# All eight PSUM banks in one ring, tiled products merged into seven runs a batch, evictions spread over slots

## The chip, the cores and the metric

The kernel runs on one core of one Trainium2 chip. The metric is device time in microseconds (us) of a whole execution. Medians are of several executions. TensorE is PE in the profile, VectorE DVE, ScalarE ACT, GpSimd POOL; PEld is the weight load.

## The reference

Eight batches, eight heads, 576 positions. `phi` gives, through a softmax over the positions, 32 memory slots a head; attention runs from `q` to those slots; its output goes through a bilinear feed-forward layer.

```python
a = softmax(phi, axis=seq)                       # 8 x 8 x 576 x 32
k_m, v_m = einsum('bhsm,bhsd->bhmd', a, k), einsum('bhsm,bhsd->bhmd', a, v)
x = softmax(scale * q @ k_m.T) @ v_m             # to 4608 x 512
out = ((x @ w_a) * (x @ w_b)) @ w_out            # d_ff 1536, out 4608 x 512 float32
```

## The kernel before

TensorE writes its products to PSUM, which this kernel uses as eight banks. An eviction is the copy of a bank to SBUF by ACT or DVE; after it the bank can be used again. A ring hands its banks out in turn.

For each batch the kernel multiplies `v_m` into `w_a` and `w_b` first (the "folds", which write `vab`), so the up products work on the 32-slot weights of each head. A batch is prepared by small products on parts of the TensorE array: sums over positions (`pkv`), transposes (`pT`), scores, denominators (`pD`), folds (`pva`). They are slipped between the full-array products of the batch before: `up` (pa, pb) and `down` (po). I call the up loops of batches 0 to 7 the first to eighth loop, and the piece between the second and the third loop, where batch 2 is finished with down products alone as filler, the stretch.

```python
ps_up = ctx.enter_context(tc.tile_pool(name="ps_up", bufs=2, space=bass.MemoryType.PSUM))   # pa, pb: 2 banks each
ps_any = ctx.enter_context(tc.tile_pool(name="ps_any", bufs=1, space=bass.MemoryType.PSUM)) # 4 banks in a ring
# ...
def fold(lo, hi, z, on_act=(True, False)):
    pvas = [banks.tile([P, 512], F32, name="pva") for _ in range(2)]
    for j in range(4):
        for g in range(2):
            nc.tensor.matmul(pvas[g][32 * j:32 * j + 32, 0:hi - lo], ..., tile_position=(64 * r, 32 * j))
    for g in range(2):      # evicted at once, one on ACT, one on DVE
        ...
# ...
for x in "qt2 sc0 qt3 sc1 va0a va0b dn va1a va1b nr0 va2a nr1 va2b nr2 - nr3 -".split():   # the stretch
    run(2, x)
    work.advance(2)         # two down products after each
every = "qt0 exp0 qt1 exp1 qt2 kv0 kv1 - kvt sc0 qt3 sc1 - va0a dn va0b nr0 va1a nr1 va1b nr2 va2a nr3 va2b"
for b in range(2, B):
    ups(steps(b, 0, NFF), named(b + 1, every) if b + 1 < B else (), (work.ready - work.done) / (2 * NFF))
```

The softmax here doesn't subtract the row's maximum and nothing guards it: scores larger than these inputs give would overflow.

## Time and profile before

| what | value |
|---|---|
| device time, median | 270.53 us (270.46 to 270.94, 3 runs) |
| span of the profile | 268.7 us |
| PE busy | 258.4 us, 96% |
| DVE, ACT busy | 62%, 50% |
| first product of the second, third loop | 55.26, 85.48 us |
| last product ends (its start plus 0.216 us), span ends | 263.3, 268.65 us |

The PE share counts products that overlap (a down product lasts 0.38 us on average, and the next can start 0.216 us after it). So it says that PE seldom stands without work, but not what PE spends. That is read from starts: the difference between two starts in the timeline is what a product or a run of products costs.

### The profile page before, as it was taken

What the parts mean: (1) busy time and instruction counts of PE and PEld (TensorE: products, weight loads), DVE (VectorE), ACT (ScalarE), POOL (GpSimd) and SP (SyncE); (2) the same over time, 40 slices, a digit from 0 to 9 for tenths busy, and PEclk for the clock granted to TensorE, in tenths of its full rate; (3) what the DMA queues carried; (4) which work ended last, traced back from release to release, by engine and by line L of the source; (5) the groups of instructions that cost most, each with busy time, mean ns of one, the idle gap of its engine ahead of it and who ended that gap; (6) DMA issues with size and microseconds to landing.
All of it is one profiled execution on the core that took longest, in us unless ns stands there. A gap on an engine that the chain in (4) does not pass through costs nothing.

```text
span 268.7 us, 7200 instructions
## 1 busy us (share of the span) xinstructions
PE 258.4 (96%) x2912; PEld 138.9 (52%) x2912; DVE 166.4 (62%) x366; ACT 135.4 (50%) x331; POOL 36.5 (14%) x59
## 2 busy tenths in 40 slices
PE   8979989999999999999999999999999999999992
PEld 3435553446534655655555545555565555666540
DVE  7544864479857679855885477846884577444100
ACT  3126752278454565726663645646573564544220
POOL 8943332100210310121003100000000000000000
PEclk9998999999999999999999999999999999999999
DMA  7999999999993595169515971111111111112243
GB/s 159 195 198 207 253 207 224 236 295 232 217 204 90 130 189 117 41 139 208 117 25 154 187 159 41 39 41 41 39 41 40 43 41 39 40 41 67 62 109 78
DMA packets 25858, 33.50 MB, mean 125 GB/s; under 512 B 1888, under 2 KB 20320, under 8 KB 25824
## 3 DMA queue, kind: packets, MB, share of 16 engines
q0 software_dynamic: 19536, 23.01, 47.6%
q1 hardware_dynamic: 6288, 10.03, 14.7%
q8 instruction: 23, 0.38, 0.5%
q14 instruction: 11, 0.09, 0.1%
HBM read 42.47 MB, written 9.44 MB: 193 GB/s over the span
## 4 chain that ended last, share of the span: by engine, by line
PE 84%; DMA 10%; DVE 2%; issue 1%; POOL 1%; ACT 1%; ACTq 0%; DVEq 0%; POOLq 0%
PE po L385 34%; PE pa L455 19%; PE pb L464 17%; DMA wb_sb<-in_moe_w_b_dram 6%; PE pva L341 6%; DMA kv_sb<-in_v_dram 4%; PE pkv L216 2%; PE pscore L296 2%; PE pR L327 1%; PE pT L245 1%; PE pD L315 1%; PE pT L251 1%; POOL q_sb L90 1%; DVE qT L203 1%; DVE ht L467 0%
## 5 line engine op out<-in xcount | busy, mean ns | idle before, releaser
L385 PE MATMUL po<-wo_sb,ht 128*128 128x512 f16 x432 | 120.4, 379 | 0.0
L467 DVE TENSOR_TENSOR ht<-a_sb,pb 128x288 f16<-128x288 f16 x192 | 77.9, 446 | 35.1 <-PE pb L464 31.2
L458 ACT CAST a_sb<-pa 128x288 f16<-128x288 f32 x192 | 67.7, 407 | 35.7 <-PE pa L455 35.2
L455 PE MATMUL pa<-A,vab 128*128 128x288 f16 x384 | 64.1, 289 | 0.5 <-ACT a_sb L458 0.5
L464 PE MATMUL pb<-A,vab 128*128 128x288 f16 x384 | 63.8, 288 | 0.3
L385 PEld LDWEIGHTS <-ht 128*128 128x128 f16 x432 | 40.8, 98 | 24.2 <-issue 2.5
L351 ACT CAST vab<-pva 128x512 f16<-128x512 f32 (+1 forms) x54 | 29.5, 555 | 43.0 <-PE pva L341 42.7
L455 PEld LDWEIGHTS <-vab 128*128 128x128 f16 x384 | 33.0, 98 | 25.2 <-issue 11.8
L464 PEld LDWEIGHTS <-vab 128*128 128x128 f16 x384 | 35.2, 98 | 18.2 <-ACT vab L351 1.2
L353 DVE CAST vab<-pva 128x512 f16<-128x512 f32 x46 | 31.6, 688 | 8.4 <-PE pva L341 7.9
L394 ACT ACTIVATE o_sb<-po 128x512 f32<-128x512 f32 (+1 forms) x36 | 21.8, 605 | 21.0 <-PE po L385 21.0
L305 ACT ACTIVATE E<-pscore,rphi 128x288 f16<-128x288 f32 x32 | 14.3, 497 | 25.3 <-PE pscore L296 25.3
L203 DVE STREAM_TRANSPOSE qT<-q_sb 128x576 f16<-128x576 f16 x32 | 24.0, 763 | 0.0
L330 DVE SCALAR_TENSOR_TENSOR A<-E,rphi,pR 128x288 f16<-128x288 f16 x32 | 16.0, 512 | 8.2 <-PE pR L327 7.5
L341 PEld LDWEIGHTS <-kvT 64*32 64x32 f16 x400 | 6.0, 89 | 19.3 <-issue 18.1
L119 PE MATMUL pw<-warm 128*128 128x512 f16 (+1 forms) x48 | 13.4, 415 | 1.3 <-DVE warm L113 1.3
L78 POOL DMA_DIRECT2D phi_sb<-in_phi_dram x7 | 5.3, 755 | 67.4 <-ACT exp_sb L194 35.5
L319 DVE RECIPROCAL rD<-pD 128x144 f16<-128x144 f32 x8 | 8.4, 1056 | 6.9 <-PE pD L315 6.8
L231 DVE CAST kvm<-pkv 128x128 f16<-128x128 f32 (+1 forms) x16 | 4.0, 265 | 13.3 <-PE pkv L216 13.3
L194 ACT ACTIVATE exp_sb<-phi_sb 128x576 f16<-128x576 f32 x16 | 10.9, 696 | 2.6 <-DMA phi_sb<-in_phi_dram 2.6
L341 PE MATMUL pva<-wa_sb,kvT 64*32 64x512 f16 (+1 forms) x200 | 10.5, 378 | 0.3 <-DVE rD L319 0.3
L341 PE MATMUL pva<-wb_sb,kvT 64*32 64x512 f16 (+1 forms) x200 | 10.6, 382 | 0.1
(44 smaller groups left out, 108.0 us busy)
## 6 DMA issues: line engine op xcount, KB each, us to landing
out_dram<-o_sb SPq DMA_DIRECT2D x72, 128.0 KB, 2.4
kv_sb<-in_v_dram POOLq DMA_DIRECT2D x8, 576.0 KB, 10.3
phi_sb<-in_phi_dram POOLq DMA_DIRECT2D x7, 576.0 KB, 5.7
kv_sb<-in_k_dram POOLq DMA_DIRECT2D x7, 576.0 KB, 7.6
q_sb<-in_q_dram POOLq DMA_DIRECT2D x6, 576.0 KB, 10.2
wo_sb<-in_moe_w_out_dram POOLq DMA_DIRECT2D x3, 512.0 KB, 17.0
q_sb<-in_q_dram POOLq DMA_DIRECT2D x4, 288.0 KB, 12.5
wa_sb<-in_moe_w_a_dram POOLq DMA_DIRECT2D x2, 512.0 KB, 13.8
```

The costliest lines, as they stand in the source:

```text
L203: nc.vector.transpose(out=t["qT"][:, hp, :], in_=qs[b][:, hp, :])
L305: nc.scalar.activation(out=Ev[:, g, :, z, :], in_=pss[z], func=AF.Exp, scale=t["rphi"][:, g:g + 1])
L330: nc.vector.scalar_tensor_tensor(out=attn[b][:, g, sl], in0=t["E"][:, g, sl], scalar=t["rphi"][:, g:g + 1], in1=pR, op0=ALU.mult, op1=ALU. ...
L341: nc.tensor.matmul(pvas[g][32 * j:32 * j + 32, 0:hi - lo], t["kvT"][64 * r:64 * r + 64, 4 + g, M * j:M * j + M], w_sbs[z][64 * r:64 * r + ...
L351: nc.scalar.copy(out=vabs[b][z][:, g, lo:hi], in_=pvas[g][:, 0:hi - lo])
L353: nc.vector.tensor_copy(out=vabs[b][z][:, g, lo:hi], in_=pvas[g][:, 0:hi - lo])
L385: nc.tensor.matmul(po, hts[pair][:, i, P * c:P * (c + 1)], wo_sb[:, i, :], start=(i == 0), stop=(i == NFF - 1))
L394: nc.scalar.mul(out=o_sb[:, :cut], in_=po[:, :cut], mul=1.0 / (CS * CS))
L455: nc.tensor.matmul(pa, vab[0][:, g, fs], A[:, g, HALF * hf:HALF * (hf + 1)], start=(g == 0), stop=(g == 1))
L458: nc.scalar.copy(out=a_sb, in_=pa)
L464: nc.tensor.matmul(pb, vab[1][:, g, fs], A[:, g, HALF * hf:HALF * (hf + 1)], start=(g == 0), stop=(g == 1))
L467: nc.vector.tensor_tensor(out=ht[:, i, t0:t0 + HALF], in0=a_sbs[hf], in1=pb, op=ALU.mult)
```

## The change

Its intent: fewer switches between the full array and its tiles. A merged run needs up to four free banks at once, so all eight banks become one ring in which a tile can be held; the evictions are taken out of the runs and put in slots of their own; the last down block is cut in two halves and stored from two queues; loads and early products of batch 1 are reordered.

```diff
-    ps_up = ctx.enter_context(tc.tile_pool(name="ps_up", bufs=2, space=bass.MemoryType.PSUM))
-    ps_any = ctx.enter_context(tc.tile_pool(name="ps_any", bufs=1, space=bass.MemoryType.PSUM))
+    psum = ctx.enter_context(tc.tile_pool(name="psum", bufs=1, space=bass.MemoryType.PSUM))   # order 0..7
+    load_wo(0)                          # now ahead of phi, k, q of batch 1
@@ v transposes: 64 array columns before, 32 now, the same tile shape as the k transposes
-                    for z in range(2):
-                        nc.tensor.transpose(out=pT[64 * z:64 * z + 64, 4 + g, :], in_=kvm[:, g, 1], ...)
+                    for z in range(4):
+                        nc.tensor.transpose(out=pT[32 * z:32 * z + 32, 4 + g, :], ...)
@@ folds and scores: products of both halves in one run, banks held, evictions apart
+        def fold(lo, hi, zs):
+            for z in zs:
+                t["pva", z] = [banks.take([P, 512], F32, "pva", hold=True) for _ in range(2)]
+        def take_fold(lo, hi, z): ...
@@ the stretch and the loops (x = eviction of a fold, e = exponential of scores, ' = of the batch after)
-    every = "qt0 exp0 qt1 exp1 qt2 kv0 kv1 - kvt sc0 qt3 sc1 - va0a dn va0b nr0 va1a nr1 va1b nr2 va2a nr3 va2b"
+    for f in slots(2, "qt2 qt3 sc+e0 e1 v0+x0a x0b dn v1+x1a x1b+exp0' nr0 v2+x2a exp1'+x2b nr1 qt0' nr2 qt1' nr3 qt2' qt3'"):
+        f()
+        work.advance(1.5)
+    every = "kv - kvt sc+e0 - e1 v0+x0a x0b dn exp0' qt0' v1+x1a x1b exp1' nr0 qt1' nr1 v2+x2a x2b qt2' nr2 - nr3 qt3'"
@@ the last down block
+    last_down(B // 2 * NI - 1)          # 2 x 12 products of 256 columns, evictions of 128, stores from two queues
```

## The prediction

> **What bounds the kernel now.** I read the page's busy shares, then the busy time of each engine in hand-chosen stretches (one per phase), then the TensorE timeline in the steady part, then the chain that ended last. Page, part 1, then three stretches (start:end, length, busy us and instructions per engine, clock, DMA):
>
> ```profile
> PE 258.4 (96%) x2912; PEld 138.9 (52%) x2912; DVE 166.4 (62%) x366; ACT 135.4 (50%) x331; POOL 36.5 (14%) x59
> ...
> 55.26:71.70 16.44, 16.28 (x229) 10.28 (x221) 14.15 (x34) 12.29 (x32) 2.23 (x3) 1.00 1.13 264
> 71.70:85.48 13.78, 13.21 (x132) 4.63 (x130) 9.53 (x17) 6.33 (x12) 0.74 (x1) 1.00 0.87 156
> 85.48:109.00 23.52, 23.52 (x311) 13.53 (x310) 18.59 (x43) 14.46 (x37) 2.98 (x4) 1.00 0.68 132
> 164.50:194.00 29.50, 29.50 (x342) 16.46 (x340) 20.52 (x45) 16.25 (x41) 0.00 (x0) 1.00 0.20 45
> ```
>
> From 85 us on TensorE (PE) never stops: 23.52 of 23.52 us, at full clock. So VectorE (DVE), ScalarE (ACT) and DMA are not the bound there, and only PE time removed counts. But busy does not mean streaming. The timeline shows it; its columns are start, busy us, engine, line, products:
>
> ```profile
> 167.63 0.81 PE L385 MATMUL po<-wo_sb,ht 128*128 128x512 f16 x3
> 168.37 0.41 PE L341 MATMUL pva<-wb_sb,kvT 64*32 64x512 f16 x8
> 168.72 0.66 PE L455 MATMUL pa<-A,vab 128*128 128x288 f16 x4
> ...
> 172.90 0.59 PE L385 MATMUL po<-wo_sb,ht 128*128 128x512 f16 x2
> 173.33 0.65 PE L464 MATMUL pb<-A,vab 128*128 128x288 f16 x4
> 173.82 0.59 PE L385 MATMUL po<-wo_sb,ht 128*128 128x512 f16 x2
> 174.35 0.61 PE L216 MATMUL pkv<-kv_sb,exp_sb 64*32 64x192 f16 x40
> 174.89 0.30 PE L455 MATMUL pa<-A,vab 128*128 128x288 f16 x1
> ```
>
> Read starts, not durations. Two down products take 173.33-172.90 = 0.43 us, 0.215 each. Before a tiled run there is more: the pair at 173.82 needs 0.43 but the next start is 0.53 later, so 0.10 is lost entering. The 40 pkv products on eight array tiles are five passes of 192 columns, about 0.41 us at full clock; they take 174.89-174.35 = 0.54, so 0.13 is lost leaving. The pva run agrees: three downs take 0.74 instead of 0.645 (0.095), and eight products that stream together in 0.216 take 0.35 (0.13). So each excursion from full-array to tiled products costs about 0.22 us, whatever its size. The chain of what ended last begins with loads and ends with two evictions and a store:
>
> ```profile
> 4.25 9.96 DMA kv_sb<-in_v_dram
> 14.49 16.21 DMA wb_sb<-in_moe_w_b_dram
> ...
> 263.56 0.39 ACT o_sb L394
> 263.96 0.02 issue
> 263.98 0.42 DVE o_sb L396
> ```
>
> The last weights land at 14.49+16.21 = 30.7 us; the fold that needs them runs at 30.75. Up to there the start is paced by loads.
>
> **What the Trainium skill says.** "TensorEngine Tiling (Array Packing)", Key Properties: changing the tiling mode, not merely the tile, drains TensorE. The trace agrees: 0.10 us in, 0.13 out. "TensorE: Matmul & The Clock Gate", Back-to-back issue gap: N/2.4+2.5 ns warm; here 512 columns take 215 ns and 288 columns 0.49/4 = 122 ns, so it agrees and I use it for content. "TensorEngine Tiling", PSUM Bottleneck: use both ScalarE and VectorE for evacuation; the folds already do (L351 586 ns on ACT, L353 688 ns on DVE for 512 columns), so spreading them saves no engine time, it only avoids bunching. "Trainium Kernel Development and Optimization", Key Constraints: all issuing queues share the same DMA engines, so a second queue saves issue time alone; this bears on the last store.
>
> **The change part by part.**
>
> 1. *Seven runs a batch.* Before, a batch has kv sums in two runs, transposes, scores in two, folds in six, denominators: 12 runs, and the transposes change mode inside (128*32 to 128*64). In mode changes: 11x2+3 = 25. After: kv, kvt (one mode), sc, three folds, dn: 7 runs, 14 changes. Eleven changes at 0.11 us = 1.2 us a batch. Merging adds no array work: the same products, and inside pkv the passes already follow each other at streaming pace, so I expect a merged fold (16 products) to take about 0.22+0.35 = 0.57 us from its start to the next. Counted in the built instruction order, the whole program goes from 210 to 136 mode changes: 66 saved in batches 2 to 7, six in batch 1 (six folds become three), two elsewhere. Total 74 x 0.11 = 8.1 us of PE time. Five batches (3 to 7) are prepared inside the loops that start at 85 us, where PE is 100% busy: 5 x 1.2 = 6.0 us on the path.
>
> 2. *One ring of eight banks.* Before, each pa and pb had its own two banks. Now a merged fold holds four and a score pair four, a down one, so pa/pb share three until the first evictions. Going through the built order, the shortest distance from a bank's last product to its reuse is about 1.06 us in the first loop (the one with the fewest downs between) and about 1.3 to 1.5 us later; two evictions need about 0.1+2x0.41 = 0.9 us. So nearly hidden: I charge 0.4 us in all.
>
> 3. *Batch 1 and the order of loads.* wo part 0 comes before phi of batch 1, and the exponentials of batch 1 leave the first up loop. Before, ACT waits 2.6 us there for phi, and PE 0.52 us for a_sb. Four filler products (0.88 us) go, since wo part 0 no longer lands only at 40.4 us (issued 23.41, 17.0 to landing). Against it: ks-kt now follow each other with nothing between, two waits of about 0.45 us for kvm. Adding products in their order from 37.1 us I get the second up loop starting at 54.6 instead of 55.26.
>
> 4. *Second up loop and the stretch after it.* PE content falls by about 0.8 us (two fold runs, one kv run, one transpose change), and some of the 1.1 us that PE waits there may go; but DVE is busy 14.15 of 16.44 us, so the loop cannot go much below 15.2: it ends near 69.9 instead of 71.70. The stretch after holds 28 downs instead of 40, 2.6 us less that comes back in the next loop. Its folds lose three runs and scores one, but sc still waits for two transposes (1.36 us in the chain before) and DVE now carries two more transposes of batch 3 ahead of the last normalise. In DVE order: 1.4 transposes, 1.3 idle for the first fold, 3.6 fold evictions, 1.0 reciprocal, 1.7 normalise, 1.4 next transposes, plus 0.9 of start-up and gaps: about 11.3 us, equal to the old 13.78-2.6 = 11.2. So no gain here: the third loop starts near 81.2, which with the postponed 2.6 counts as 83.8 against 85.48: 1.7 us for parts 3 and 4.
>
> 5. *Tail.* Before: last product starts 263.10, ACT 0.38 then DVE 0.42 in turn, stores issued at 264.43 and 264.94 from one queue, landing 267.3. After: 128 columns each instead of 256 (about 0.28 each, an estimate from 384 ns for 256 and 611 for 512), saving 0.25, and the second store leaves from ACT's queue, saving about 0.5. Twice 12 products of 256 columns stream as long as 12 of 512. Gain 0.7.
>
> Sum: 6.0 - 0.4 + 1.7 + 0.7 = 8.0 us: 270.53 - 8.0 = 262.5.
>
> **Rivals.**
>
> *The ring turns into a wait.* A slow eviction blocks every later user of the ring, and a merged fold asks for four banks at once. For: 1.06 us of distance in the first loop; DVE already 18.59 of 23.52 there. Against: PE had no waits with only two banks per kind and distances of 1.17 us. If each of the 15 merged folds and five score runs lost 0.2 us, 4 us are gone: 266.5.
>
> *Merged runs do not stream.* If the second half of a fold, which reloads weights into tiles still in use, pays an exposed load of about 0.1 us (98 ns a load in the groups), half of the saving on folds and scores goes: 264.5. Against: the pkv passes do not pay it.
>
> *The middle stays DVE-bound.* If the stretch from 55 to 84 us gains nothing: 263.9. The opposite also exists: scores of the two groups use complementary array tiles, so a merged sc may overlap and save 0.1 us a batch more, and the wider ring may take out all waits of the second loop: 261.
>
> **Range and chances.** The 6.0 us is counted on a saturated engine with measured costs; I trust it to 1.5 us. Start and middle may be off by 1.5 either way, the tail by 0.3. That gives 260.2 to 265.4. Two per cent is 265.1, so only the first rival at full size, or two smaller ones together, keep it within 2%. Nothing could make it slower by 5 us unless waits appear in every loop.
>
> **What would show it.** Right: between 80 and 245 us PE still 100% busy; a fold run of 16 products whose start to next start is about 0.57 us; each loop shorter by 1.2 us apart from its downs; pa and pb with under 0.5 us waiting on ACT or DVE; last store landing about 3.1 us after the last product ends (3.9 before: 263.1+0.3 to 267.3). Wrong: waits of pa, pb or pva on a_sb, vab or ht evictions in the waits view; fold runs over 0.65 us; a third up loop starting after 83 us; DVE above 95% in a loop.

## The result

| | before | after |
|---|---|---|
| device time, median | 270.74 us (4 runs) | 258.16 us (257.53 to 258.58, 4 runs) |
| ratio of fast runs | 1 | 0.9532 (0.9507 to 0.9557) |
| span of the profile | 268.65 us | 256.29 us |

A ratio is the mean time of one kernel's fast runs over that of the other's in the same rounds, so it is not quite the ratio of the medians. The kernel got 12.6 us faster. The prediction said 8.0 us, and the result lies below its range.

**Where the time went.** I cut both traces at the first pa product of each loop. The down products in each piece are counted in the built instruction order, and one costs 0.216 us (512 columns, start to next start).

| piece | before, us (downs) | after, us (downs) | difference | net of moved downs |
|---|---|---|---|---|
| start to second loop | 55.26 | 54.15 | -1.11 | -1.11 |
| second loop and stretch | 30.22 (34) | 25.60 (28) | -4.62 | -3.33 |
| third loop | 23.50 (25) | 23.87 (32) | +0.37 | -1.14 |
| fourth loop | 28.68 (49) | 27.00 (48) | -1.68 | -1.46 |
| fifth, sixth, seventh loop | 31.06, 28.46, 31.06 | 29.60, 27.00, 29.60 | -1.46 each | -1.46 each |
| eighth loop and last downs | 35.08 | 35.10 | +0.02 | +0.02 |
| last product to the end | 5.34 | 4.37 | -0.97 | -0.97 |

The differences add up to the 12.36 us between the spans. The profile after, part 1 of its page (busy us and share):

```profile
PE 244.5 (95%) x2952; PEld 139.2 (54%) x2952; DVE 165.3 (64%) x371; ACT 133.9 (52%) x328; POOL 36.6 (14%) x59
```

PE is busy for 13.9 us less, while DVE and ACT stay within 1.5 us of what they had. The stretches after (start:end, length, then PE, PEld, DVE, ACT, POOL busy; granted clock, DMA share, GB/s):

```profile
54.15:68.90 14.75, 14.75 (x225) 10.45 (x225) 13.75 (x35) 11.77 (x32) 2.24 (x3) 1.00 1.17 259
68.90:79.75 10.85, 10.08 (x126) 3.81 (x124) 9.14 (x16) 7.29 (x15) 1.50 (x2) 1.00 1.18 237
79.75:103.62 23.87, 23.71 (x321) 14.27 (x320) 19.82 (x46) 15.03 (x38) 2.98 (x4) 1.00 0.78 171
160.22:187.23 27.01, 27.01 (x338) 15.84 (x337) 19.63 (x44) 16.01 (x40) 0.00 (x0) 1.00 0.17 40
```

The second loop takes 14.75 us and PE is busy for all of it, where the prediction expected DVE to hold it at 15.2. A merged fold in the timeline after, two halves in one run:

```profile
98.14 0.41 PE L343 MATMUL pva<-wa_sb,kvT 64*32 64x512 f16 x8
98.36 0.40 PE L343 MATMUL pva<-wb_sb,kvT 64*32 64x512 f16 x8
98.69 0.66 PE L476 MATMUL pa<-A,vab 128*128 128x288 f16 x4
```

The second half starts 0.22 us after the first, at streaming pace; only then are 0.33 us spent on the second half and on leaving. The run takes 98.69-98.14 = 0.55 us, as the prediction expected (0.57). The scores, before and after:

```profile
149.94 0.44 PE L296 MATMUL pscore<-qT,kvT 32*32 32x288 f16 x16
150.31 0.67 PE L455 MATMUL pa<-A,vab 128*128 128x288 f16 x4
```

```profile
108.93 0.49 PE L293 MATMUL pscore<-qT,kvT 32*32 32x288 f16 x32
109.35 0.66 PE L476 MATMUL pa<-A,vab 128*128 128x288 f16 x4
```

Before, 16 products take 0.37 us. After, 32 products take 0.42. A group is two passes of 288 columns at 0.122 us, or 0.245 us, so 0.42 is less than two groups one after the other (0.49) before anything is added for leaving: the two groups overlap. This is a gain that the sum of the prediction did not contain.

The chain that ended last, after: the load of the last weights, and the two evictions of the last half block.

```profile
14.86 15.92 DMA wb_sb<-in_moe_w_b_dram
...
252.18 0.28 ACT o_sb L423
...
252.48 0.29 DVE o_sb L424
```

The weights land at 30.8 us as before (30.7), so the start is still paced by loads. The evictions take 0.28 and 0.29 us instead of 0.39 and 0.42.

### The profile page after: what moved, and what is told of

It reads as the page before. It is cut to its first block, busy times and chain, and to the rows that moved or that the text cites. A ratio compares the mean times of both kernels' runs of the same rounds, so it can differ in the third digit from the quotient of the medians.

```text
span 256.3 us, 7288 instructions
## 1 busy us (share of the span) xinstructions
PE 244.5 (95%) x2952; PEld 139.2 (54%) x2952; DVE 165.3 (64%) x371; ACT 133.9 (52%) x328; POOL 36.6 (14%) x59
## 3 DMA queue, kind: packets, MB, share of 16 engines
q0 software_dynamic: 19536, 23.01, 49.8%
## 4 chain that ended last, share of the span: by engine, by line
PE 83%; DMA 10%; DVE 3%; POOL 1%; issue 1%; ACTq 0%; ACT 0%; DVEq 0%; POOLq 0%
PE po L393 34%; PE pb L485 18%; PE pa L476 18%; DMA wb_sb<-in_moe_w_b_dram 6%; PE pva L343 5%; DMA kv_sb<-in_v_dram 4%; PE pkv L217 2%; DVE qT L203 2%; PE pR L328 1%; PE pscore L293 1%; PE pT L241 1%; PE pD L316 1%; POOL q_sb L89 1%; PE pl L421 1%; DVE rD L320 0%
## 5 line engine op out<-in xcount | busy, mean ns | idle before, releaser
L393 PE MATMUL po<-wo_sb,ht 128*128 128x512 f16 x420 | 117.4, 379 | 0.0
L393 PEld LDWEIGHTS <-ht 128*128 128x128 f16 x420 | 39.9, 98 | 23.0 <-issue 2.7
L476 PEld LDWEIGHTS <-vab 128*128 128x128 f16 x384 | 35.6, 98 | 26.3 <-issue 6.7
L485 PEld LDWEIGHTS <-vab 128*128 128x128 f16 x384 | 34.7, 98 | 18.9 <-issue 1.7
L355 ACT CAST vab<-pva 128x512 f16<-128x512 f32 (+1 forms) x50 | 27.9, 582 | 23.0 <-PE pva L343 23.0
L355 DVE CAST vab<-pva 128x512 f16<-128x512 f32 (+1 forms) x50 | 31.9, 663 | 10.7 <-PE pva L343 10.2
L400 ACT ACTIVATE o_sb<-po 128x512 f32<-128x512 f32 x35 | 21.4, 611 | 17.7 <-PE po L393 17.7
L143 PE MATMUL pw<-warm 128*128 128x512 f16 (+1 forms) x44 | 10.9, 386 | 1.3 <-DVE warm L112 1.3
L343 PE MATMUL pva<-wb_sb,kvT 64*32 64x512 f16 (+1 forms) x200 | 9.8, 369 | 1.0 <-DMA wb_sb<-in_moe_w_b_dram 1.0
L81 POOL DMA_DIRECT2D kv_sb<-in_k_dram x9 | 6.7, 747 | 27.5 <-PE pb L485 24.4
L343 PEld LDWEIGHTS <-kvT 64*32 64x32 f16 x400 | 4.0, 89 | 11.2 <-issue 8.9
## 6 DMA issues: line engine op xcount, KB each, us to landing
q_sb<-in_q_dram POOLq DMA_DIRECT2D x4, 288.0 KB, 12.6
wa_sb<-in_moe_w_a_dram POOLq DMA_DIRECT2D x2, 512.0 KB, 13.9
```

Of the source, the lines that this page charges most:

```text
L143: nc.tensor.matmul(pw[:, :cols], warm[:, :P], warm[:, :cols], start=True, stop=True)
L343: nc.tensor.matmul(t["pva", z][g][0][32 * j:32 * j + 32, 0:hi - lo], t["kvT"][64 * r:64 * r + 64, 4 + g, M * j:M * j + M], w_sbs[z][64 * r ...
L355: engine_copy(out=vabs[b][z][:, g, lo:hi], in_=pva[:, 0:hi - lo])
L393: nc.tensor.matmul(po, hts[pair][:, i, P * c:P * (c + 1)], wo_sb[:, i, :], start=(i == 0), stop=(i == NFF - 1))
L400: nc.scalar.mul(out=o_sb, in_=po, mul=1.0 / (CS * CS))
L476: nc.tensor.matmul(pa, vab[0][:, g, fs], A[:, g, HALF * hf:HALF * (hf + 1)], start=(g == 0), stop=(g == 1))
```

## The experiments

Twelve runs were made, of eleven kernels, all with correct outputs. From the third loop on, the pieces of one program repeat from run to run to 0.03 us, so I read effects there. In the second loop they do so in all but two runs: in e2 and e9 the sums of batch 2 took 1.22 and 1.16 us instead of 0.87, and DVE waited 0.5 and 0.3 us there for the load of q.

The start does not repeat: seven profiled kernels with the same instructions up to the second loop (the changed one and six experiments) began it between 53.08 and 56.19 us. Two things vary there. The fold that waits for the last weights began between 29.75 and 31.84 us. From it to the second loop six of the seven took 23.32 or 23.33 us; e8 took 24.99, with the clock halved for 3.4 us of it (below). So the start is read from this fold on, and differences of less than 1 us in whole times are not argued from. "End" in the table is from the end of the last product (its start plus its streaming time) to the end of the span. The runs e5, e7, b1 and b2 are told in the text.

| run | median, us | ratio to before | second loop and stretch | third | fifth loop | end |
|---|---|---|---|---|---|---|
| before | 270.74 | 1 | 30.22 | 23.50 | 31.06 | 5.34 |
| after | 258.16 | 0.9532 | 25.60 | 23.87 | 29.60 | 4.37 |
| e1_ring_alone | 267.43 | 0.9889 | 27.97 | 23.50 | 31.06 | 5.32 |
| e2_folds_apart | 261.86 | 0.9681 | 26.80 | 24.39 | 30.28 | 4.35 |
| e3_scores_apart | 260.00 | 0.9621 | 25.38 | 24.29 | 30.01 | 4.37 |
| e4_scores_side_by_side | 257.77 | 0.9538 | 25.59 | 23.84 | 29.57 | 4.37 |
| e9_v_transpose_wide_again | 258.97 (1 run) | - | 26.01 | 23.99 | 29.72 | 4.37 |
| e6_tail_as_before | 259.33 | 0.9587 | 25.59 | 23.87 | 29.60 | 5.33 |
| e8_evict_at_once | 258.68 | 0.9585 | 25.59 | 24.13 | 29.60 | 4.35 |
| e10_downs_ahead_of_scores | 257.39 | 0.9534 | 25.59 | 23.01 | 29.60 | 4.37 |

### The ring alone

Theory A: the gain is fewer changes of mode, and the ring only makes them possible. Rival B: the ring itself took away waits. The kernel before gets the eight-bank ring and nothing else.

```diff
-            pa = ps_up.tile([P, HALF], F32, name="pa")
+            pa = banks.tile([P, HALF], F32, name="pa")      # same for pb, po, pw; Banks over 8 tags
```

> The kernel before with all eight PSUM banks in one ring and nothing else changed. Theory A (fewer changes of tiling mode are the gain, the ring only makes them possible): loops from 85 us on stay as long as before to 0.1 us, because TensorE had no waits there; only the second up loop (16.44 us before, about 1.1 us of waits by start-to-start) may lose up to 0.9 us. Total 269.8 to 270.8. Rival B (the ring itself took away waits and is worth several us): 267 or less.

Measured: 267.43 us, 3.15 us less than before on the same chip. Neither side was right as it stood. In the loops from the third on the ring is worth nothing, as A says: 23.50, 28.68 and 31.06 us before and with the ring. But the second loop and the stretch lose 2.25 us. Before, the stretch in the timeline reads (in brackets: idle before, and what ended it)

```profile
75.87 0.63 PE L341 MATMUL pva<-wb_sb,kvT 64*32 64x512 f16 x8
76.43 0.61 PE L385 MATMUL po<-wo_sb,ht 128*128 128x512 f16 x2
...
77.75 0.39 PE L341 MATMUL pva<-wa_sb,kvT 64*32 64x512 f16 x1
78.44 0.41 PE L341 MATMUL pva<-wa_sb,kvT 64*32 64x512 f16 x7 [0.31 <-DVE rD L319]
78.78 0.61 PE L385 MATMUL po<-wo_sb,ht 128*128 128x512 f16 x2
```

and with the ring, the fold that took 1.03 us and the one after it

```profile
76.14 0.41 PE L341 MATMUL pva<-wa_sb,kvT 64*32 64x512 f16 x8
76.49 0.61 PE L385 MATMUL po<-wo_sb,ht 128*128 128x512 f16 x2
77.02 0.41 PE L341 MATMUL pva<-wb_sb,kvT 64*32 64x512 f16 x8
77.36 0.60 PE L385 MATMUL po<-wo_sb,ht 128*128 128x512 f16 x2
```

Before, a fold took 0.56 us (76.43-75.87), and one took 1.03 (78.78-77.75), because its second bank was the one that the reciprocal of the denominators still read (going through the order in which the code hands out banks gives this): with one bank held by a down product, three were left, and a fold takes two. With the ring each fold takes 0.34 to 0.35 us. The stretch goes from 13.78 to 12.23 us with the same products, the second loop from 16.44 to 15.74. The piece from the fold on the last weights to the second loop goes from 24.51 to 24.02.

### Folds apart

```diff
-    "... v0+x0a x0b dn exp0' qt0' v1+x1a x1b ..."
+    "... v0a+x0a v0b+x0b dn exp0' qt0' v1a+x1a v1b+x1b ..."      # batches 2 to 7
```

> The changed kernel with each merged fold of batches 2 to 7 taken apart again into its two halves in neighbouring slots: 18 more runs, 36 more changes of mode, same products and evictions. Theory A: 0.22 us for each extra run, so 0.66 us more in each of the loops 3 to 7 and 3.3 to 4.0 us in all (258.2 to about 262). Rival (merged folds gain by something else, such as evictions in another order): loops grow by less than 0.3 us each, or by more than 1.

Measured: 261.86 us. The fourth to seventh loops are 0.68 to 0.69 us longer each, the third 0.52: three more runs at 0.23 us. That is theory A at its predicted size. In the third loop the first pa products also wait 0.16 us less than in the changed kernel for the last normalise (0.65 us to the next start against 0.81), which makes up the difference. The 26.80 us of the table holds 0.51 us that is not an effect: it lies in the second loop, whose program is the same (see above); the stretch itself is 0.69 us longer.

### Scores apart and side by side

```diff
-    "kv - kvt sc+e0 - e1 ..."
+    "kv - kvt s0+e0 s1 e1 ..."
```

> The changed kernel with the two score groups of batches 2 to 7 in slots of their own again: 6 more runs. If only the change of mode costs: 0.22 us each, 1.3 us in all. If the merged run also overlaps the two groups on complementary array tiles (0.42 us for 32 products against 2 x 0.37 before): 0.41 us each, 2.1 us in the five loops and 2 to 2.5 us in all.

Measured: each loop from the third on is 0.41 to 0.43 us longer. An excursion costs 0.22 by itself, so the other 0.2 us is overlap of the two groups inside the merged run. In the stretch the opposite holds: 25.38 against 25.60 us, since the first group no longer stands in one run with the second, which waits for transposes there.

```diff
-            for g in gs:                      # both halves of a group, then the next group
-                for dh in range(2):
+            for dh in range(2):               # first halves of both groups, then second halves
+                for g in gs:
```

> The changed kernel with the score products of both groups issued half by half (first halves of both groups, then second halves). If the two groups run side by side on complementary tiles, a run of 32 products shrinks from 0.42 to about 0.37 us, 0.3 us in all, near the noise, so it is read from the run's start to next start. If the array serialises the groups the run stays at 0.42 or grows to 0.62.

```profile
109.90 0.46 PE L294 MATMUL pscore<-qT,kvT 32*32 32x288 f16 x32
110.29 0.66 PE L477 MATMUL pa<-A,vab 128*128 128x288 f16 x4
```

Measured: the run takes 110.29-109.90 = 0.39 us instead of 0.42, and the loops are 0.02 to 0.03 us shorter, as little as pieces repeat to, but in every loop from the third to the seventh. So the array does not serialise the groups, and it overlaps them nearly as well when they are issued one after the other.

### The transposes

```diff
-                    for z in range(4):   # 32 columns
+                    for z in range(2):   # 64 columns, as before the change
```

> The changed kernel with the v transposes on 64 array columns again, which puts a change of mode inside the transpose run. Theory A: 0.12 us more a batch, about 0.7 us in all, and the same 0.12 in each loop from the third on. If a change between two tiled modes is free: no difference.

The profile of this run: a span of 408.4 us at a mean clock of 0.56. Of its four timed runs the fast ones have a ratio of 0.9571. That says little about 0.7 us.

> The same kernel as in the run with wide v transposes, once more, because its profile fell in the slow state (clock 0.56). Read by stages only: 0.12 us more in each of the loops 3 to 7 if a change between two tiled modes costs as much as leaving to full-array products; 0 if it is free.

```profile
107.95 0.41 PE L241 MATMUL pT<-ident,kvm 128*32 128x128 f16 x16
108.28 0.30 PE L247 MATMUL pT<-ident,kvm 128*64 128x128 f16 x4
108.52 0.66 PE L484 MATMUL pb<-A,vab 128*128 128x288 f16 x4
```

The same place in the changed kernel, where both transposes have one tile shape:

```profile
107.45 0.41 PE L241 MATMUL pT<-ident,kvm 128*32 128x128 f16 x16
107.69 0.28 PE L247 MATMUL pT<-ident,kvm 128*32 128x128 f16 x8
107.90 0.66 PE L485 MATMUL pb<-A,vab 128*128 128x288 f16 x4
```

The first 16 transposes take 0.33 us to the next start where the tile shape changes, and 0.24 where it does not; the v transposes after them take 0.24 against 0.21. Each loop from the third on is 0.12 us longer: a change from one tiled shape to another costs about what leaving does (0.13). The second loop of this run is 0.41 us longer, of which 0.29 is the wait at the sums told above.

### The end

```diff
-    last_down(B // 2 * NI - 1)
+    for _ in down(B // 2 * NI - 1):      # one block of 512 columns, evictions of 256, both stores from one queue
+        pass
```

> The changed kernel with the old ending: the last down block as twelve products of 512 columns, two evictions of 256 columns and both stores from one queue. By the spans of before and after the time from the end of the last product to the end of the span went from 5.33 to 4.38 us, so 0.9 to 1.0 us more here, all of it after the last product; by the prediction 0.7.

Measured: 5.33 us from the end of the last product to the end of the span, against 4.37, and all other pieces unchanged. The new ending is worth 0.96 us.

### The order of loads

```diff
-    load_wo(0)
     load_phi(1)
```

> The changed kernel with the load order of before: wo part 0 after phi, k and q of batch 1, so landing near 40.4 instead of 33.4 us. The first eight early downs stand at 37.1 us and wait for it: 2 to 3 us longer up to the second up loop (start at 56 to 57.5 instead of 54.15), part of which the later waits in that stretch (about 0.9 us) can absorb. If loads play no role: no difference.

Measured: 263.17 us, ratio 0.9726. The second loop starts at 59.88 us, later than I expected. The timeline, and two stretches, one inside the wait and one of the products after it (0.57 and 0.50 are the granted clock):

```profile
40.45 3.59 PE L392 MATMUL po<-wo_sb,ht 128*128 128x512 f16 x8 [3.33 <-DMA wo_sb<-in_moe_w_out_dram]
```

```profile
39.00:40.00 1.00, 0.00 (x0) 0.00 (x0) 0.00 (x0) 0.00 (x0) 0.05 (x1) 0.57 1.22 202
40.40:43.90 3.50, 3.45 (x8) 1.03 (x8) 0.00 (x0) 0.00 (x0) 0.75 (x1) 0.50 1.24 207
```

PE waits 3.33 us for the weights (37.12 to 40.45), and inside the wait the clock is halved: the records show it at 0.50 from 39.13 us, 2.0 us after the last product, to 45.96, 6.8 us in all. Eight down products take 3.52 us (40.45 to 43.97) instead of 1.82. The wait was predicted; what it does to the clock was not. All later pieces are those of the changed kernel. So the early use of wo pays only with the new order of loads: from the fold on the last weights to the second loop this run takes 29.16 us against 23.33, of which 3.5 is the later start of the first down product and 2.3 the slower products after it.

The kernel before takes 24.51 us for that piece and the ring alone 24.02, so the change gains 1.18 us there, 0.49 of it by the ring. The other 0.69 is the new order of loads and early products together with one merged fold; their shares were not separated.

### Evictions at once

```diff
-    "... sc+e0 - e1 v0+x0a x0b dn ... v1+x1a x1b ..."
+    "... sc+e0+e1 - - v0+x0a+x0b - dn ... v1+x1a+x1b - ..."
```

> The changed kernel with the evictions of a merged fold and of a score pair all in the slot of their products instead of spread over two or three slots. If spreading matters, pa and pb wait for banks behind four evictions (about 1.2 us of ACT and 1.3 us of DVE in a row): up to 0.3 us a fold, 1 to 4 us in all. If the slack of the ring is enough: within 0.3 us of the changed kernel.

Measured: the third loop is 0.26 us longer (one merged fold takes 0.82 us to the next start instead of 0.56), every other piece is unchanged. So spreading the evictions is worth 0.26 us in the one loop with the fewest downs, and nothing where more of them stand between. Its profiled execution took 260.61 us, the other three 258.63 to 258.74, because it also holds a late start (56.19 us), which does not count against this:

```profile
31.20 0.41 PE L343 MATMUL pva<-wb_sb,kvT 64*32 64x512 f16 x8 [2.00 <-DMA wb_sb<-in_moe_w_b_dram]
```

```profile
32.34:35.76 3.42, 3.42 (x16) 2.17 (x15) 1.87 (x5) 1.72 (x5) 1.31 (x2) 0.50 1.16 243
```

A wait of 2.00 us for the last weights was followed by the half clock, from 32.34 to 35.76 us, and the piece from that fold to the second loop is 1.67 us longer than in the other six.

### Downs ahead of the scores, and a version that beats both

In the changed kernel, apart from the first 10 us, these are the longest waits of PE that are left (who waited for whom, total us, times, longest):

```profile
PE pscore L293 <- DVE qT L203: 1.1, 3, 0.4
PE pva L343 <- DMA wb_sb<-in_moe_w_b_dram: 1.0, 1, 1.0
PE pT L277 <- DVE kvm L270: 0.7, 2, 0.3
...
```

No line names an eviction of pa, pb or a fold. This view lists only idle time of PE, not a product that waits once it has started, so the starts count too: in the fourth loop each of the 24 groups of pa or pb takes 0.49 or 0.50 us to the next start, and each pair of downs 0.43, or 0.53 before a tiled run. So the ring holds nobody up there.

```diff
+    for n, f in enumerate(slots(2, "qt2 qt3 sc+e0 ...")):
         f()
-        work.advance(1.5)
+        work.advance(3.5 if n < 2 else 1.5)
```

> The changed kernel with four more down products moved from the third up loop to the place just before the scores of batch 2, where TensorE waited about 0.8 us for the query transposes. Theory: a down product costs 0.216 us wherever TensorE is full, so the third loop gets 0.86 us shorter, and the stretch before it gets longer by only 0.1 us, because the products fill the wait: 0.7 to 0.8 us less by stages. Rival (the stretch is bound by VectorE): the wait only moves to the end of the stretch, and nothing is gained.

Measured: the stretch with the second loop stays at 25.59 us with four more products in it, and the third loop loses 0.86 us. The wait was filled, and the outcome that the rival named, a wait at the end of the stretch, did not come. This does not mean that VectorE bounds nothing in the stretch: the scores end 2.61 us after its start in both kernels (68.90 to 71.51 us, and 68.77 to 71.38), so up to there the query transposes on VectorE set the pace, and four products fit in at no cost. After the scores neither timeline shows a wait of PE before the third loop.

The last two kernels add the other fillings: folds of batch 0 where their weights have landed, downs between the k sums and their transposes, the later transposes of queries after the last normalise, denominators in one run with the second fold; in the second one also four pieces in the last block.

```diff
-    ups(steps(0, 4, 12), slots(0, "- v2a+x2a - v2b+x2b"))
+    ups(steps(0, 4, 12), slots(0, "- - - v2a+x2a - - v2b+x2b"))
-    run(1, "ks0 kt0 qt0 qt1"); some(4)
+    run(1, "ks0"); some(2); run(1, "kt0 qt0 qt1"); some(2)       # same for ks1, kt1
-    "... x0b dn exp0' qt0' v1+x1a x1b ..."
+    "... x0b - exp0' qt0' dn+v1+x1a x1b ..."
```

> A version meant to beat both: the changed kernel with downs ahead of the scores, the third transpose after the last normalise, the last two folds of batch 0 moved to where their weights have landed (1.4 us of waits), downs between the k sums and their transposes (two waits of 0.33 us), denominators in one tiled run with the second fold, score halves side by side. Estimate by stages: 1.3 us at the start, 0.6 in the early downs, 0.8 in the stretch, 0.3 in the third loop, 0.1 in each loop: 3 to 3.5 us under the changed kernel, about 255.

> The same with the last down block in four pieces of 128 columns, each in a bank of its own, so that ScalarE evicts one while TensorE computes the next, and only one eviction of 0.29 us is left after the last product: 0.25 to 0.3 us less between the last product and the end (4.37 us in the changed kernel). If 128-column products are held by weight loads instead of streaming (56 ns each), the last block takes 0.5 to 1 us longer and eats it.

Measured: 256.51 us (ratio 0.9479, 0.9456 to 0.9503) and 255.94 us (0.9462, 0.9439 to 0.9485). Both beat the changed kernel, but by 1.7 and 2.2 us (1.4 and 1.9 by the ratios, since the rounds were others), not by the expected 3 to 3.5. By pieces, the third loop gives 1.28 us, of which 0.32 are taken back in the stretch. The start, from which I had expected nearly 2 us, gives 0.86 from the fold on the last weights (22.47 and 22.48 us against 23.33): the timeline of the first one shows PE waiting 0.94 us for the second part of wo at 43.5 us, so the waits removed earlier came back at a later load. Putting the denominators beside a fold, together with the score halves side by side (0.02 to 0.03 by the run above), gave 0.14 us in the fifth and seventh loops and cost 0.04 in the fourth and sixth. In the fourth, the pa group right after that run takes 0.68 us to the next start instead of 0.49, while the reciprocal of the denominators still runs on DVE; that this is a wait for its bank was not tested. The end of the second kernel:

```profile
247.65 2.69 PE pl L424 x48
...
250.43 0.29 DVE o_sb L429
```

Forty-eight products of 128 columns take 2.69 us, 56 ns each, so they stream, and one eviction is left after them: 4.10 us from the last product to the end instead of 4.37.

## Why the prediction was wrong

The direction, and the mechanism of its largest term, were right; four of its five terms were too small and the fifth, the ring, had the wrong sign. Against the spans, 12.36 us gained stand against 8.0 predicted. The missing 4.4 us are 1.0 in part 1, 0.4 in part 2, 0.5 in part 3, 2.3 in part 4 and 0.3 in part 5.

- **Part 1, seven runs a batch: right mechanism, too small.** The traces count 210 and 136 changes of mode, as the prediction did. Predicted 1.2 us a batch, 6.0 in five loops. Measured 1.46 in each of the fourth to seventh loops and 1.14 in the third (where pa waits 0.32 us), 7.0 in all. Experiments show 0.69 from the folds, 0.42 from the scores, 0.12 from the transposes; what remains, about 0.23, is the one run of sums saved. The timelines agree (0.54 and 0.46 us before, 0.87 after, and one entry of 0.10 less), but no run tested it alone. The step that failed is "Merging adds no array work": for the scores it removes some, 0.2 us a batch, 1.0 us in five loops. The prediction named this as a rival's possibility of 0.1 us and left it out of the sum.
- **Part 2, the ring: wrong sign.** The prediction charged 0.4 us. In the loops the ring costs nothing that the waits or the starts show; the 0.3 us that pa waits at the start of the third loop is for the last normalise. In the second loop and the stretch the ring gains 2.25 us by itself.
- **Part 3: right direction, too small.** Predicted 0.66, measured 1.11, or 1.18 from the fold on the last weights, which takes the spread of the loads out. The ring alone gives 0.49 of that, which the prediction did not count. The two waits for kvm are there (0.33 each, predicted 0.45), and the order of loads is what makes the early downs pay.
- **Part 4: the largest miss, 1.04 predicted against 3.33 measured.** The step that cost most, 1.3 of the 2.3 us, is a count: "28 downs instead of 40" should have read 34, since the old list has 17 entries with two downs each. So only 6 downs were postponed, and 1.3 us of real gain was put down as postponed work. The second, 0.55 us, is "DVE is busy 14.15 of 16.44 us, so the loop cannot go much below 15.2", which read a busy engine as the bound: the loop was forecast at 15.3 us and took 14.75 with DVE doing 13.75. The third, 0.45 us, is the sum in DVE order for the stretch, 11.3 us forecast and 10.85 measured; in it, that the scores wait for two transposes was right. Behind all three, waits for banks in the second loop and the stretch were not seen: the ring alone takes 2.25 us out of them. The view that showed it before the change was the bracket at 78.44 us, a fold waiting for a reciprocal that it has no use for.
- **Part 5, the end: right, 0.97 measured against 0.7;** the run with the old ending confirms 0.96. The shares of the smaller evictions and of the second queue were not tested apart.
- **The rivals.** A wait at the ring did not appear. Merged runs stream. A middle held by DVE was the wrong rival to worry about. Its opposite, named in the same paragraph and put at 261 us, is what came: the scores overlap, by 0.2 us a batch instead of 0.1, and the wider ring takes out waits.

## What to carry to other kernels

On a saturated TensorE, price each excursion to another tiling mode (here 0.22 us whatever its size) and merge small products until as few as possible are left; groups on tiles that the other leaves free can overlap almost for nothing (0.42 us for two groups of scores, 0.37 for one). When an instruction waits for one whose data it doesn't use, look for a shared PSUM bank: here more banks in one ring were worth 2.25 us by themselves, with no product moved. Before calling an engine the bound, count what the filler work really is, and see whether that engine itself sits idle. A wait of PE can cost more than its length: here a wait of 3.33 us and one of 2.00 us were each followed by slower products at half the clock.

## What the Trainium skill lacked or had wrong

- "TensorEngine Tiling (Array Packing)", Key Properties, says that a change of mode drains TensorE but gives no size. Here: 0.10 us going in, 0.13 coming out, and 0.12 between two tiled shapes (128*32 to 128*64).
- The same section says that tiles operate independently; neither it nor "TensorE: Matmul & The Clock Gate", Part 3, has a figure for groups that are issued one after the other and use complementary tiles. Here 32 score products take 0.42 us issued by group and 0.39 interleaved, where 16 alone take 0.37.
- "TensorE: Matmul & The Clock Gate", Part 1, has the clock at half after at least one idle window of about 3.4 us. Here less was enough: in the run with the old loads the clock fell 2.0 us after the last product, in the run with evictions at once 1.1 us after the end of a wait of 2.00 us; in both, PE was busy for 1.4 us of the 3.4 us before the fall. The half clock lasted 6.8 and 3.4 us; in the first case the eight products after the wait took 1.7 us more.
- No page says how much a start paced by loads varies: in seven profiles of the same instructions the fold that waits for the last weights began between 29.75 and 31.84 us.
